# Attention on one core: output stores held back by seven pairs, the last store halved, and a new order of work in quad 2

## The chip, the cores and the metric

One core of one Trainium2 chip. The time is device microseconds of one execution; the figure for a kernel is the median of several executions. Smaller is better.

## The reference

For 16 x 32 = 512 heads, with 192 queries, 1024 keys and a head dimension of 128, all in bf16:

```python
scale = q.shape[-1] ** -0.5
scores = jnp.einsum("bhqd,bhkd->bhqk", q, k) * scale
p = jax.nn.softmax(scores, axis=-1)
return jnp.einsum("bhqk,bhkd->bhqd", p, v)
```

## The kernel before

The 512 heads are taken four at a time: 128 *quads* (NQ), numbered x. Each quad is three *steps*, so there are NF = 384 steps, numbered f or s. A quad needs 1 MB of K, 1 MB of V and 192 KB of Q, and gives 192 KB of output. Scores are computed with the keys on the partitions, so that the exponentials can go into the second matmul as they are. No maximum is subtracted: the exponential is taken directly, and the row sums come from a column of ones beside V. A check of the reciprocals of these sums decides at the end, by one number in `redo`, whether a slower general path has to run after all. With these inputs it is skipped.

What each engine does, in the order written in its own block:

- **SyncE (SP)** loads. For each n in turn it issues V of quad n + 3, K of quad n + 5 and Q of quad n + 5 (L576 to L583). There are five buffers each for K, Q and V. A K load waits until VectorE has turned all three pieces of the quad that used the buffer (L545), a V load until the second matmul is through with it (L554). After the last load SP issues those output stores that ScalarE didn't (L584).
- **VectorE** turns K (`turn_k`, three pieces of a quad) and Q (`turn_q`), and normalizes the outputs (`onorm`: a reciprocal of the sums and a multiply that writes `f_ob`). At step f it does `onorm(f - 5)`, at one step the early check, and then the pieces for step f + 3.
- **GpSimd (POOL)** reorders the turned K into `f_kt` (`order(g)`, one piece) and copies V into `f_vp` beside the ones (`spread(x, i)`, i = 0 and 1 for two heads each). For each x its order is: order(3x), spread(x-1, 0), spread(x-1, 1), order(3x+1), order(3x+2) (L621 to L631).
- **TensorE (PE)** does `qk(f)` and then `pv(f - 4)`. The second matmul of a quad has no wait of its own for V. Its order alone carries it: `pv(3(x-1))` comes after `qk(3x+1)`, which needs order(3x+1), which stands behind spread(x-1, 1) on GpSimd. There is one PSUM bank for O, so `pv(s)` takes a count of `s_on` that `onorm(s-1)` has given.
- **ScalarE (ACT)** takes the exponentials, two activations a step (L838 for one bank, L841 for three), and issues the output stores by a table, `store_at`.

Outputs of two quads (a *pair*) share one slot of `f_ob` and one store of 384 KB; the last two quads are stored alone. There are NSO = 3 slots. ACT issues the store of the pair that ends before quad x + c at step 3(x + c) + 6. A slot is written again only when its store has landed (L771). The lines that set this:

```python
    stores = [(x, GQ) for x in range(0, NQ - GQ, GQ)] + [(NQ - 2, 1), (NQ - 1, 1)]
    EARLY = NF - 9
...
            store_at = {3 * (x + c) + 6: i for i, (x, c) in enumerate(stores) if 3 * (x + c) + 6 < NF}
```

`EARLY` is the number of steps whose reciprocals the early check covers. Its three parts run on VectorE in steps f = EARLY + 5 to EARLY + 7, and a check of the rest comes behind the last `onorm`.

Of the kernel before, what the change touches and what calls it, by code (L numbers as in the profile page):

```python
# [30 lines left out]
def _general_path(nc, q, k, v, out, redo, hints, stored, G=16, NS=2, LAGS=(2, 4, 5, 7), ROUTES=(R_W, R_W, R_EA)):  # L31
# [16 lines left out]
    NPT = L_PV - L_EV + 2  # L48
    NSO = 2
    NRS = 4  # L50
# [4 lines left out]
    of = out.rearrange("b h s d -> (b h) s d")  # L55

    def route(u):
        return ROUTES[u % len(ROUTES)]
# [19 lines left out]
    with ExitStack() as es:  # L78
        def sb(name, shape, dt):
            return es.enter_context(nc.sbuf_tensor(name, shape, dt))  # L80
# [4 lines left out]
        def sem(name):  # L85
            return es.enter_context(nc.semaphore(name))
# [3 lines left out]
        vs = sb("vs", [128, NS, G, KT_TILES, 128], BF16)  # L90
        ob = sb("ob", [128, NSO, PPG, 4, 128], BF16)
        ss = sb("ss", [128, NSS, SK], F32)
# [13 lines left out]
        svl = [sem("svl%d" % i) for i in range(NS)]  # L106
        sst = [sem("sst%d" % i) for i in range(NSO)]
        s_qk = sem("s_qk")
# [8 lines left out]
        s_on = sem("s_on")  # L117
# [15 lines left out]
        def store_cnt(g):  # L133
            return 48 * (g // NSO + 1)

# [13 lines left out]
        def sync_general(e):  # L149
# [20 lines left out]
            def stores(g):  # L170
                so = g % NSO
                e.wait_ge(s_on, (g + 1) * PPG)
                h0 = g * G
                og = of[h0:h0 + G]
                e.dma_start(
                    og[:, 0:128, :].rearrange("h p d -> p h d"),
                    ob[:, so].rearrange("p pg (x y) d -> p (pg x) (y d)", y=2)[:, :, 0:128],
                ).then_inc(sst[so], 16)
                oab = og[:, 128:192, :].rearrange("(pg x) p d -> x p pg d", x=2)
                e.dma_start(oab[0], ob[0:64, so, :, 1, :]).then_inc(sst[so], 16)  # L180
                e.dma_start(oab[1], ob[64:128, so, :, 1, :]).then_inc(sst[so], 16)
# [3 lines left out]
            for g in range(NGR):  # L185
                if g + NS < NGR:
                    loads(g + NS)
                stores(g)
            for so in range(min(NSO, NGR)):
                n_uses = len(range(so, NGR, NSO))  # L190
                e.wait_ge(sst[so], 48 * n_uses)

        @block.sync
        def _(e):
            sync_general(e)
            stored(e)

        @block.gpsimd
        @_only_if(nc, redo, hints)
        def _(gp):  # L200
            gp.memset(ones[:], 1.0).then_inc(s_setup, 1)
            gp.wait_ge(s_setup, 1)
            gp.affine_select(
                ident[:], ones[:], [[1, 128]], ALU.is_equal, 0.0, base=0, channel_multiplier=-1
            ).then_inc(s_setup, 1)

            def shift(u):
                gp.wait_ge(s_max, u + 1)
                if u >= NX:
                    gp.wait_ge(s_tr, u - NX + 1)  # L210
                gp.tensor_tensor(
                    x_sb[:, u % NX, :], ss[:, u % NSS, :],
                    nb[:, u % NSS: u % NSS + 1].to_broadcast([128, SK]), ALU.subtract,
                ).then_inc(s_xp, 1)

            for u in range(NU):
                if route(u) == R_W:
                    shift(u)
# [202 lines left out]
def _attention_kernel(nc, q, k, v, out):  # L421
# [9 lines left out]
    NF = 3 * NQ  # L431
# [5 lines left out]
    AHEAD = 3  # L437
    NKN, NVS, NKT, NVP = 5, 5, 2, 2
    GQ = 2
    NSO = 3  # L440
    VB = 136

    qf = q.rearrange("b h s d -> (b h) s d")
# [2 lines left out]
    of = out.rearrange("b h s d -> (b h) s d")  # L446

    stores = [(x, GQ) for x in range(0, NQ - GQ, GQ)] + [(NQ - 2, 1), (NQ - 1, 1)]
    EARLY = NF - 9

    with ExitStack() as outer:
        redo = outer.enter_context(nc.sbuf_tensor("redo", [1, 1], mybir.dt.int32))

        def sem(name):
            return outer.enter_context(nc.semaphore(name))
# [8 lines left out]
        s_st = [sem("f_st%d" % i) for i in range(NSO)]  # L464
# [3 lines left out]
        s_vp = sem("f_vp")  # L468
# [5 lines left out]
        s_rc = sem("f_rc")  # L474
        s_pf = sem("f_pf")
        s_on = sem("f_on")
        s_fin = sem("f_fin")
        s_fl = sem("f_fl")

        with ExitStack() as es:  # L480
            def sb(name, shape, dt):
                return es.enter_context(nc.sbuf_tensor(name, shape, dt))
# [16 lines left out]
            ob = sb("f_ob", [128, NSO, GQ * 6, D], BF16)  # L499
# [15 lines left out]
            def store(e, i):  # L515
                so = i % NSO
                x, c = stores[i]
                if x + c == NQ:
                    e.wait_ge(s_fin, 1)
                else:  # L520
                    e.wait_ge(s_rc, 3 * (x + c) + 1)
                e.dma_start(
                    of[4 * x:4 * x + 4 * c].rearrange("(a x) (p j) d -> (x p) a (j d)", x=2, j=3),
                    ob[:, so, 0:6 * c, :].rearrange("p (a j) d -> p a (j d)", j=3),
                ).then_inc(s_st[so], 16)


            store_at = {3 * (x + c) + 6: i for i, (x, c) in enumerate(stores) if 3 * (x + c) + 6 < NF}

            def load_q(e, x):  # L530
                e.dma_start(
# [53 lines left out]
                    store(e, i)  # L585
            def stored(e):
                for so in range(NSO):
                    e.wait_ge(s_st[so], 16 * len(range(so, len(stores), NSO)))

            @block.gpsimd  # L590
            def _(gp):
                gp.memset(ones[:], 1.0).then_inc(s_one, 1)  # L592

                def set_v(part):
                    return gp.memset(part.bitcast(U32), 0x3F803F80)  # L595

                set_v(vp[:, 0, 0:2 * T].rearrange("p a d -> p (a d)")).then_inc(s_set, 1)
                set_v(vp[:, 0, 2 * T:].rearrange("p a d -> p (a d)")).then_inc(s_blank, 1)
                set_v(vp[:, 1].rearrange("p a d -> p (a d)"))

                def order(g):
                    x, b = divmod(g, 3)
                    lo, hi = PIECES[b]
                    gp.wait_ge(s_kx, g + 1)
                    if x >= NKT - 1 and b == 0:
                        gp.wait_ge(s_qk, 3 * (x - NKT) + 3 + PRE)
                    gp.tensor_copy(  # L607
                        kt[:, x % NKT].bitcast(U32).rearrange("p U (j s u) c -> p U j s (u c)", s=2, u=2)[:, lo:hi],
                        kx[:, x % 2].rearrange("p (U s j u) -> p U j s u", s=2, j=32, u=2)[:, lo:hi],
                    ).then_inc(s_kt, 1)  # L610

                def spread(x, i):
                    if i == 0:
                        gp.wait_ge(s_v[x % NVS], 16 * (x // NVS + (2 if x % NVS == 0 else 1)))
                        gp.wait_ge(s_pv, 3 * (x - NVP) + 3 + BLANK)
                    gp.tensor_copy(  # L616
                        vp[:, x % NVP, 2 * T * i: 2 * T * i + 2 * T, 0:D].bitcast(U32),
                        vs[:, x % NVS, 2 * i: 2 * i + 2, :].rearrange("p a (t d) -> p (a t) d", d=D).bitcast(U32),
                    ).then_inc(s_vp, 1)

                for x in range(NQ + 1):  # L621
                    if x == NQ // 2:
                        hint(gp)
                    if x < NQ:
                        order(3 * x)
                    if x >= 1:
                        for i in range(2):
                            spread(x - 1, i)
                    if x < NQ:
                        order(3 * x + 1)  # L630
                        order(3 * x + 2)  # L631

            @block.tensor
# [84 lines left out]
            def _(dve):  # L718
# [4 lines left out]
                for z in range(2):  # L723
                    ins = clear(low[:, z, :, 1, :])
# [4 lines left out]
                for z in range(2):  # L729
                    ins = clear(low[:, z, :, 2, :])  # L730
# [30 lines left out]
                def onorm(s):  # L761
                    x, w = divmod(s, 3)
                    i, a = where[x]
                    so = i % NSO
                    ri = rinv[:, 2 * s: 2 * s + 2]
                    dve.wait_ge(s_pv, s + 1 + BLANK)
                    O = o_of(s)
                    dve.reciprocal(ri, O[:, :, 128]).then_inc(s_rc, 1)  # L768
                    dve.wait_ge(s_rc, s + 1)
                    if a == 0 and w == 0 and i >= NSO:  # L770
                        dve.wait_ge(s_st[so], 16 * (i // NSO))  # L771
                    dve.tensor_tensor(  # L772
                        ob[:, so, 6 * a + 2 * w: 6 * a + 2 * w + 2, :],
                        O[:, :, 0:128],
                        ri.unsqueeze(2).to_broadcast([128, 2, D]),
                        ALU.mult,
                    ).then_inc(s_on if s < NF - 1 else s_fin, 1)

                cnt = [0]

# [17 lines left out]
                for f in range(NF + LAG + 1):  # L798
                    s = f - LAG - 1
                    if f == NF // 2:  # L800
                        hint(dve)
                    if s >= 0:
                        onorm(s)
                        if 0 <= s - EARLY < 3:
                            check(0, 2 * EARLY, 0, s - EARLY)
                    g = f + AHEAD
                    if 5 <= g < NF:
                        x, b = divmod(g, 3)
# [3 lines left out]
                for part in range(3):  # L812
                    check(2 * EARLY, 2 * NF, 1, part)
                dve.sem_inc(s_fl, 1)  # L814
# [69 lines left out]
```

## Time and profile before

| | |
|---|---|
| Median of 4 runs | 818.04 us (817.12 to 819.3) |
| Profiled execution | 816.57 us, span 814.8 us |
| PE busy | 800.9 us, 98% |
| ACT busy | 749.9 us, 92% |
| VectorE busy | 604.5 us, 74% |
| GpSimd busy | 552.0 us, 68% |
| Moved by DMA | 319.16 MB, mean 392 GB/s |
| Loads of K, V and Q, issue to landing (median) | 18.1, 16.3, 14.2 us |
| Stores issued by ACT, issue to landing (median) | 9.5 us, 62 of 384 KB |

The profile is one execution. An engine is busy while one of its instructions runs; time in which it waits is put down to whatever released it, as far as the profile shows it. The DMA share is the mean over the core's 16 DMA engines, and can come out slightly above 1. Queue q1 is SP's, q10 is ACT's. In a timeline the columns are start and duration in us, engine, line, operation, output and input, and in brackets the idle time before it and what ended that.

### The profile page before, as it was taken

To read this page: it belongs to the slowest core of one execution; us is meant where nothing else is said; L and a number is where in the kernel's file an instruction comes from. 1 tells how busy PE (TensorE), PEld (TensorE's weight loads), DVE (VectorE), ACT (ScalarE), POOL (GpSimd) and SP (SyncE) were. 2 spreads that over 40 slices of the span, in tenths; PEclk is the share of its full clock that TensorE was granted. 3 is DMA by queue.
4 is the path that set the end of the run, shared out by engine and by line. 5 is a ranking of instruction groups with operands and counts; after the bars stand their busy time and mean duration, and the time that the engine had idled before them with its cause. 6 is when DMAs were issued, how large, how long until landed. Compare 5 with 4: busy or idle time off the path is not lost. (4 is left out here: it accounts for less than half of the span.)

```text
span 814.8 us, 71454 instructions
## 1 busy us (share of the span) xinstructions
PE 800.9 (98%) x32996; PEld 714.1 (88%) x32996; DVE 604.5 (74%) x1293; ACT 749.9 (92%) x772; POOL 552.0 (68%) x648
## 2 busy tenths in 40 slices
PE   8999999999999999999999999999999999999997
PEld 6888888888888888888888888888888888888886
DVE  4777777777777777777777777777777777777775
ACT  7999999999999999999999999999999999998995
POOL 5776767667667767766766676676666766766674
PEclk9999999999999999999999999999999999999999
DMA  8999999999999999999999999999999999999992
GB/s 290 402 406 407 407 406 406 408 405 405 408 404 406 407 404 407 407 403 407 408 403 409 407 403 408 407 404 394 398 407 401 401 408 396 390 407 387 389 379 69
DMA packets 138454, 319.16 MB, mean 392 GB/s; under 512 B 7216, under 2 KB 56368, under 8 KB 122160
## 3 DMA queue, kind: packets, MB, share of 16 engines
q1 hardware_dynamic: 105536, 294.22, 92.0%
q10 hardware_dynamic: 32880, 24.58, 9.0%
q14 instruction: 32, 0.26, 0.1%
q8 instruction: 6, 0.10, 0.1%
HBM read 293.60 MB, written 25.17 MB: 391 GB/s over the span
## 5 line engine op out<-in xcount | busy, mean ns | idle before, releaser
L841 ACT ACTIVATE f_pt<-f_s 128x1536 bf16<-128x1536 f32 x384 | 554.6, 1444 | 0.0
L654 PE MATMUL f_s<-f_qt,f_kt 32*128 32x192 bf16 (+1 forms) x20528 | 422.0, 226 | 7.2 <-PEq L637 6.4
L683 PE MATMUL f_o<-f_vp,f_pt 128*64 128x129 bf16 x12368 | 425.8, 222 | 1.8 <-PEq L637 1.0
L683 PEld LDWEIGHTS f_o<-f_vp,f_pt 128*64 128x64 bf16 x12368 | 362.8, 110 | 51.1 <-issue 24.8
L616 POOL COPY f_vp<-f_vs 128x1024 uint32<-128x1024 uint32 x256 | 260.1, 1045 | 208.0 <-DMA f_vs<-in_v_dram 202.0
L654 PEld LDWEIGHTS f_s<-f_qt,f_kt 32*128 32x128 bf16 x20528 | 348.4, 92 | 44.1 <-issue 9.8
L747 DVE STREAM_TRANSPOSE f_kx<-f_kn 128x768 uint32<-128x768 uint32 (+1 forms) x384 | 335.1, 873 | 59.0 <-DMA f_kn<-in_k_dram 55.0
L607 POOL COPY f_kt<-f_kx 128x768 uint32<-128x768 uint32 (+1 forms) x384 | 295.2, 788 | 44.1 <-DVE f_kx L747 39.2
L838 ACT ACTIVATE f_pt<-f_s 128x512 bf16<-128x512 f32 x384 | 229.5, 598 | 56.4 <-PE f_s L654 15.4
L772 DVE TENSOR_TENSOR f_ob<-f_o,f_rinv 128x256 bf16<-128x256 f32 x381 | 161.8, 425 | 13.3 <-DVE f_rinv L768 0.3
L768 DVE RECIPROCAL f_rinv<-f_o 128x2 f32<-128x2 f32 x381 | 63.7, 167 | 132.7 <-PE f_o L683 130.6
L756 DVE STREAM_TRANSPOSE f_qt<-f_qn 128x384 uint32<-128x384 uint32 x128 | 73.0, 570 | 0.0
L825 ACT ACTIVATE f_pt<-f_ones 128x1536 f32<-128x1536 bf16 x3 | 4.2, 1473 | 0.0
L595 POOL MEMSET f_vp<- 128x1088 uint32 (+1 forms) x3 | 3.8, 1311 | 0.0
L683 PE MATMUL f_s<-f_vp,f_pt 128*64 128x129 bf16 x96 | 3.2, 220 | 0.2 <-issue 0.2
L683 PEld LDWEIGHTS f_s<-f_vp,f_pt 128*64 128x64 bf16 x96 | 2.9, 110 | 0.4 <-issue 0.4
L825 ACT ACT_TABLE_LOAD x1 | 1.3, 1283 | 1.2 <-PEq L869 1.2
L696 PE MATMUL f_o<-f_ones 128*128 128x512 bf16 x2 | 1.0, 620 | 1.1 <-POOL f_ones L592 1.1
L720 DVE MEMSET f_pt<- 128x256 uint32 x4 | 1.1, 272 | 0.9 <-PEq L869 0.9
L768 DVE RECIPROCAL f_rinv<-f_s 128x2 f32<-128x2 f32 x3 | 0.5, 171 | 1.4 <-PE f_s L683 1.4
L713 PE MATMUL f_o<-f_bad,f_ones 128*1 128x1 bf16 x1 | 0.2, 165 | 1.3 <-DVEq L814 1.3
L713 PEld LDWEIGHTS f_o<-f_bad,f_ones 128*1 128x1 bf16 x1 | 0.1, 80 | 1.4 <-DVEq L814 1.4
(15 smaller groups left out, 6.9 us busy)
## 6 DMA issues: line engine op xcount, KB each, us to landing
f_kn<-in_k_dram SPq DMA_DIRECT2D x127, 1024.0 KB, 18.1
f_vs<-in_v_dram SPq DMA_DIRECT2D x127, 1024.0 KB, 16.3
f_qn<-in_q_dram SPq DMA_DIRECT2D x127, 192.0 KB, 14.2
out_dram<-f_ob ACTq DMA_DIRECT2D x62, 384.0 KB, 9.5
f_vs<-in_v_dram SPq DMA_DIRECT2D x2, 512.0 KB, 6.5
f_kn<-in_k_dram SPq DMA_DIRECT2D x2, 512.0 KB, 4.6
out_dram<-f_ob SPq DMA_DIRECT2D x1, 384.0 KB, 3.7
out_dram<-f_ob SPq DMA_DIRECT2D x2, 192.0 KB, 2.2
```

Of the source, the lines that this page charges most:

```text
L595: return gp.memset(part.bitcast(U32), 0x3F803F80)
L607: gp.tensor_copy(kt[:, x % NKT].bitcast(U32).rearrange("p U (j s u) c -> p U j s (u c)", s=2, u=2)[:, lo:hi], kx[:, x % 2].rearrange("p (U ...
L616: gp.tensor_copy(vp[:, x % NVP, 2 * T * i: 2 * T * i + 2 * T, 0:D].bitcast(U32), vs[:, x % NVS, 2 * i: 2 * i + 2, :].rearrange("p a (t d) ...
L654: ins = pe.matmul(S[:, c0: c0 + n1 - n0], kt[r, x % NKT, 2 * t + h, :, c], qt[r, x % R, h, n0:n1, c], start=w == 0 and g == 0, stop=w == 3 ...
L683: ins = pe.matmul(O[64 * z: 64 * z + 64, u, 0:129], pt[:, x % R, 2 * y + z, t * SQ + 64 * j: t * SQ + 64 * j + 64], vp[:, x % NVP, (2 * y ...
L747: dve.transpose(kx[:, x % 2].rearrange("p (U s j u) -> p s u U j", s=2, j=32, u=2)[:, :, :, lo:hi], kn[:, x % NKN].rearrange("p (s u U i) ...
L756: dve.transpose(qt[:, x % R].bitcast(U32).rearrange("p b (y j u) c -> p u y b (j c)", y=3, u=2), qn[:, x % NKN].rearrange("p (u y b i) -> ...
L768: dve.reciprocal(ri, O[:, :, 128]).then_inc(s_rc, 1)
L772: dve.tensor_tensor(ob[:, so, 6 * a + 2 * w: 6 * a + 2 * w + 2, :], O[:, :, 0:128], ri.unsqueeze(2).to_broadcast([128, 2, D]), ALU.mult,). ...
L825: return act.activation(part.bitcast(F32), ones[:, 0:1].to_broadcast([128, 2 * T * SQ // 2]), ACT_FN.Copy)
L838: act.activation(pt[:, x % R, 0, c], s1_ps[:], ACT_FN.Exp, scale=scale).then_inc(s_e1, 1)
L841: act.activation(pt[:, x % R, 1:4, c], s3_ps[f % 2][:], ACT_FN.Exp, scale=scale).then_inc(s_e3, 1)
```

## The change

Five things change.

1. `f_ob` gets ten slots. ACT's stores come 42 steps, seven pairs, later (`HOLD`), and none is put on ACT after step NF - 12. SP issues the remaining ones after its last load: nine pairs and the two single quads, where it issued one pair and the two singles.
2. The store of the last quad becomes two, of two heads each; `s_fin` counts the last two steps in place of the last one.
3. `EARLY` goes from NF - 9 to NF - 33.
4. In quad 2 (`HELD`) GpSimd does order(7) ahead of the two spreads of quad 1. Since `qk(7)` no longer implies that V is there, VectorE holds back the count of `s_on` that `pv(3)` takes: after `onorm(2)`'s multiply it waits for that multiply and for the first spread of quad 1, and only then adds to `s_on`.
5. In the general path, GpSimd also waits for the stores (`stored(gp)`).

```diff
@@ general path, GpSimd
+            stored(gp)
             gp.memset(ones[:], 1.0).then_inc(s_setup, 1)
@@ constants
-    NSO = 3
+    NSO, HOLD = 10, 7
+    HELD = 2
...
-    EARLY = NF - 9
+    EARLY = NF - 33
...
+        s_held = sem("f_held")
@@ store(e, i)
                 if x + c == NQ:
-                    e.wait_ge(s_fin, 1)
-                else:
-                    e.wait_ge(s_rc, 3 * (x + c) + 1)
+                    for y in range(2):
+                        e.wait_ge(s_fin, y + 1)
+                        e.dma_start(
+                            of[4 * x + 2 * y:4 * x + 2 * y + 2].rearrange("x (p j) d -> (x p) (j d)", j=3),
+                            ob[:, so, 3 * y:3 * y + 3, :].rearrange("p j d -> p (j d)"),
+                        ).then_inc(s_st[so], 16)
+                    return
+                e.wait_ge(s_rc, 3 * (x + c) + 1)
...
-            store_at = {3 * (x + c) + 6: i for i, (x, c) in enumerate(stores) if 3 * (x + c) + 6 < NF}
+            store_at = {3 * (x + c) + 6 + 6 * HOLD: i for i, (x, c) in enumerate(stores)
+                        if 3 * (x + c) + 6 + 6 * HOLD <= NF - 12}
@@ stored(e)
-                    e.wait_ge(s_st[so], 16 * len(range(so, len(stores), NSO)))
+                    last = (len(stores) - 1) % NSO == so
+                    e.wait_ge(s_st[so], 16 * (len(range(so, len(stores), NSO)) + last))
@@ GpSimd's loop
                     if x < NQ:
                         order(3 * x)
+                    if x == HELD:
+                        order(3 * x + 1)
                     if x >= 1:
                         for i in range(2):
                             spread(x - 1, i)
                     if x < NQ:
-                        order(3 * x + 1)
+                        if x != HELD:
+                            order(3 * x + 1)
                         order(3 * x + 2)
@@ onorm(s)
-                    dve.tensor_tensor(
+                    ins = dve.tensor_tensor(
...
-                    ).then_inc(s_on if s < NF - 1 else s_fin, 1)
+                    )
+                    if s == 3 * (HELD - 1) - 1:
+                        ins.then_inc(s_held, 1)
+                        dve.wait_ge(s_held, 1)
+                        dve.wait_ge(s_vp, 2 * HELD - 1)
+                        dve.sem_inc(s_on, 1)
+                    else:
+                        ins.then_inc(s_on if s < NF - 2 else s_fin, 1)
```

## The prediction

> **What bounds the kernel now.** I read the slices of the page first, then the waits of the steady stretch, then the timelines of single engines.
>
> ```profile
> PE 800.9 (98%) x32996; PEld 714.1 (88%) x32996; DVE 604.5 (74%) x1293; ACT 749.9 (92%) x772; POOL 552.0 (68%) x648
> q10 hardware_dynamic: 32880, 24.58, 9.0%
> out_dram<-f_ob SPq DMA_DIRECT2D x1, 384.0 KB, 3.7
> out_dram<-f_ob SPq DMA_DIRECT2D x2, 192.0 KB, 2.2
> ```
>
> PE and ACT are both nearly full, so every hole in them is lost for good. Stretches of the windows view (us, busy time of each engine, clock, DMA share, GB/s) show the transfers at their limit too, until the loads are through:
>
> ```profile
> 37.00:122.00 85.00, 85.00 (x3540) 76.00 (x3538) 63.82 (x140) 80.30 (x84) 58.32 (x69) 1.00 1.04 406
> 740.00:795.00 55.00, 53.89 (x2220) 48.04 (x2216) 40.04 (x88) 50.55 (x53) 36.93 (x43) 1.00 1.00 382
> 795.00:801.00 6.00, 5.38 (x230) 4.80 (x230) 5.33 (x12) 5.47 (x6) 4.68 (x7) 1.00 0.27 90
> 801.00:815.00 14.00, 9.77 (x366) 8.70 (x354) 6.43 (x20) 5.82 (x6) 3.37 (x3) 1.00 0.20 61
> ```
>
> The last 20 us leave the DMA engines idle for four fifths. How often the shortage reaches ACT is told by the waits from 28.4 to 798.8:
>
> ```profile
> POOL f_vp L616 <- DMA f_vs<-in_v_dram: 198.8, 121, 3.1
> DVE f_kx L747 <- DMA f_kn<-in_k_dram: 44.8, 80, 1.6
> ACT f_pt L838 <- PE f_s L654: 9.6, 24, 1.0
> ```
>
> The sum of 9.6 counts overlaps, so I go by ACT's starts. From 38.63 to 239.88 it does 98 steps: 2.0536 us a step. Step 8 starts at 28.36 and step 380 at 798.75: 770.39 for 372 steps, against 372 x 2.0536 = 763.9. So 6.4 us are lost in between, in places where VectorE waited for a K load first. Steps 0 to 8 take 18.51 against 16.43: 2.1 us lost at the start. One hole comes after all K loads:
>
> ```profile
> 798.27 1.01 DVE L784 TENSOR_SCALAR f_chk<-f_rinv 128x750 f32<-128x750 f32 x1
> 799.31 0.58 DVE L756 STREAM_TRANSPOSE f_qt<-f_qn 128x384 uint32<-128x384 uint32 x1
> 801.50 0.60 ACT L838 ACTIVATE f_pt<-f_s 128x512 bf16<-128x512 f32 x1 [0.81 <-PE f_s L654]
> ```
>
> The first check stands in front of the last turn of Q, PE waits for that, and step 381 starts 2.75 after step 380: 0.70 lost, with no load to blame.
>
> [...] its V copies start when the load lands:
>
> ```profile
> 51.40 2.03 POOL L616 COPY f_vp<-f_vs 128x1024 uint32<-128x1024 uint32 x2 [1.10 <-DMA f_vs<-in_v_dram]
> 57.93 2.03 POOL L616 COPY f_vp<-f_vs 128x1024 uint32<-128x1024 uint32 x2 [1.48 <-DMA f_vs<-in_v_dram]
> 63.70 2.03 POOL L616 COPY f_vp<-f_vs 128x1024 uint32<-128x1024 uint32 x2 [1.08 <-DMA f_vs<-in_v_dram]
> 70.15 2.03 POOL L616 COPY f_vp<-f_vs 128x1024 uint32<-128x1024 uint32 x2 [1.37 <-DMA f_vs<-in_v_dram]
> 75.88 2.03 POOL L616 COPY f_vp<-f_vs 128x1024 uint32<-128x1024 uint32 x2 [0.94 <-DMA f_vs<-in_v_dram]
> ```
>
> The steps are 6.53, 5.77, 6.45, 5.73: a quad in which a pair is stored takes 0.7 to 0.8 us longer. [...]
>
> **Part 1, stores seven pairs behind.** ACT's first store goes from step 12 to step 54, about 37 to 122 us. Seven pairs of stores leave the stretch before the last loads and land after them. Each frees 0.75 us of load time (bounds: 0.69, the low end of the spacing, and 0.97, its 393 KB at 406 GB/s): 7 x 0.75 = 5.2 us, bounds 4.8 to 6.8. The loads can use it, since a K load takes 18.1 us from issue to landing, so some 18 us of work stand queued, more than 5.2. Slot reuse in ob costs nothing: a slot's store is issued 11 steps (22.6 us) ahead of its next writer as before, and lands in 9.5. ACT issues eight stores fewer; an issue there lies beside its activation, so 0.
>
> Loads that set the end come 5.2 earlier, so of the 6.4 us of holes 1.2 would stay.
>
> **Part 2, the check at step 356 (EARLY).** Its three parts (702 columns, about 0.94, 0.87, 0.87 by the 750-column rows) now stand in steps that also turn K, at about 2.05 - 1.6 = 0.45 us of free VectorE time a step. I put 0.7 to 1.2 us of hole on them, the low end by the hole at step 381, the high end adding 0.45 for the third part. But a hole ahead of a late load is paid out of the 1.2 that the loads would cost anyway; and the 0.70 after the last K load is gone. By loads the stream ends 5.2 + 0.7 = 5.9 earlier, by engines 6.4 + 0.7 - (0.7 to 1.2) - 0.1 = 5.8 to 6.3. The later holds: **-5.8 us**. The last check grows from 18 to 66 columns: 48 more at (1009 - 167) / 732 = 1.15 ns, some 0.05 us in each of three parts in series: **+0.15**.
>
> **Part 3, quad 2.** GpSimd's order(7) goes ahead of the V spread that starts at 21.59, so QK of step 7 (now 24.73, idle 0.24) may start some 0.3 earlier. I count it at nothing, since the next PV waits for something else:
>
> ```profile
> 24.55 0.98 DVE L747 STREAM_TRANSPOSE f_kx<-f_kn 128x768 uint32<-128x768 uint32 x1 [1.45 <-DMA f_kn<-in_k_dram]
> 25.62 0.42 DVE L772 TENSOR_TENSOR f_ob<-f_o,f_rinv 128x256 bf16<-128x256 f32 x1
> 26.19 1.10 PE L683 MATMUL f_o<-f_vp,f_pt 128*64 128x129 bf16 x32 [0.36 <-PEq L637]
> ```
>
> VectorE stands before the K load that lands at 24.5, so the normalization that frees the O bank ends at 26.04, and PV starts at 26.19 whatever QK did. The new wait stands after that instruction: V's half has been spread by 22.6, so it costs the semaphore's way round alone, about the 0.04 us seen between reciprocal and multiply, up to 0.1; queued behind it are the next turn of K on VectorE, and PE through s_on. Part 3: -0.3 to +0.15, value +0.1, already in the sum.
>
> **Part 4, the end.** SP, behind its last load, now issues nine pairs, a single and two halves, where it issued a pair and two singles. K of the last quad is turned at 794.72; two V loads follow, the first copied from 797.83, the second 1,049 KB later at 406 GB/s, 2.6 us: loads end near 800.4, then 795.2. A pair in a queue of stores alone is not shown. Low bound 0.75, as between loads; high bound twice the difference of the landings above, 2 x (3.7 - 2.2) = 3.0. I take the queue's own share: 9.0% of 814.8 / 62 = 1.18. Ten pairs' worth then needs 11.8 and 2 for the landing: 809.0. The last multiply, at 811.61 before, ends at 805.8; a half issued then lands near 807.9. Before, 1.0 us lay between the last landing (811.64 + 2.2) and the end of the span, and the chain of waits ran over the check and not the store. So the store is late by 1.1, of which I charge **+0.5** (0 to 1.1). That the last store is halved gains at most 0.2 and is hidden behind this: 0. The longer list of waits in stored() is a few waits already satisfied, and GpSimd's new call of it stands in the branch that is skipped: 0 to 0.1 together.
>
> **Sum.** -5.8 + 0.15 + 0.5 = -5.15. The profiled execution took 816.57 (span 814.84, 1.7 around it) and would take 811.4. It lies 1.5 under the median of the runs, 818.04; I apply the difference to the median: **812.9 us**.
>
> **Rivals.** A measurement of this kernel can tell about 0.2%, 1.6 us, from no change; "same" means within that.
>
> *Forecast*, 0.68: the credit carries to the end, 811 to 814.5.
>
> *The credit is spent early*, 0.17: the rate fell to 382 GB/s in the last stretch, and with a shortage that grows further where the check's hole is added to it, only 2 to 3.5 us remain: 814.5 to 816. For it: the holes get longer late (1.0 at most after 740). Against: lost rate costs the kernel before as much.
>
> *The engines are the bound and the holes weren't the loads'*, 0.05: then the two checks cancel, and the time stays within 1.6 us of 818.0. Against: the holes that I followed have VectorE waiting for K ahead of them.
>
> *The stores drain too slowly*, 0.10, the slower side (0.02 of it within the same band): from 795.2 the queue has 12.7 us less 2 of landing for ten pairs' worth, so from about 1.1 us a pair each 0.1 adds 1.0 us, and at about 1.7 the gain is gone. At 3.0 it would end near 795.2 + 30 + 2 = 827, and the run near 831. The landing of the lone pair after 3.7 us speaks for it; the 9.0% share and the 0.75 between loads speak against it.
>
> A last rival is that store order does nothing because the loads' rate isn't shared: the 6.53 and 5.77 exclude it.
>
> **How the numbers follow.** Faster 0.85 (forecast and spent credit), same 0.07 (the engines' case and 0.02 of the slow tail), slower 0.08. The range 810.6 to 816.2 holds the first two cases and leaves out the slow tail and the top of the credit's bound (6.8 instead of 5.2, which would be 811.3 less the missing tail cost).
>
> **What would show it.** ACT's holes against K between 122 and 720 us gone or nearly so; GpSimd's V wait far below 198.8 us; V spacing near 5.7 from 37 to 122 us; a check hole near 740 us and none at step 381; DMA share near 1 for some 10 us after the loads. Step 8 should not come sooner than 28.36. If holes against K stay at 4 us or more in sum, the credit was mis-sized; if the last landing is over 2 us behind the last multiply plus 2.2, the tail was.

## The result, and the profile after

The changed kernel takes 814.33 us (median of 42 runs, 812.3 to 818.72), the kernel before 817.07 (63 runs). The ratio is 0.9969, with a 95% interval of 0.9961 to 0.9976: 0.31% faster. The medians lie 2.7 us apart; the forecast was 5.15 us. (One of the 63 executions took 1186.45 us; the median isn't moved by it.)

In the profiled executions the span went from 814.84 to 812.07. Cut at ACT's starts and at the end of the last multiply, the 2.8 us between these two spans divide like this:

| Stretch | before, us | after, us | difference | forecast |
|---|---|---|---|---|
| to ACT's first step | 9.85 | 10.55 | +0.70 | 0 |
| step 0 to step 8 | 18.51 | 18.94 | +0.43 | +0.1 |
| step 8 to step 380 | 770.39 | 764.58 | -5.81 | -5.1 to -5.2 |
| step 380 to step 383 | 6.85 | 6.16 | -0.69 | -0.70 |
| step 383 to the last multiply's end | 6.01 | 6.97 | +0.96 | 0 |
| from there to the end of the span | 3.23 | 4.87 | +1.64 | +0.15 and +0.5 |

(The forecast's 5.8 for the middle and the check, and 0.1 of the start, are set apart here.) The middle gave what was asked of it. The start and the end took 3.7 us back, where 0.75 was reckoned with. Each column is one execution. The 1.1 us of the start turn out below to be mostly a matter of the execution, so that the sum of this table comes so near to the 2.7 us of the medians is in part chance.

The waits of the steady stretch, steps 8 to 380 of the kernel after (us in total, times, longest):

```profile
POOL f_vp L629 <- DMA f_vs<-in_v_dram: 45.7, 37, 2.3
DVE f_kx L763 <- DMA f_kn<-in_k_dram: 3.2, 10, 0.5
ACT f_pt L861 <- PE f_s L670: 2.3, 3, 1.3
```

Before, these were 198.8, 44.8 and 9.6. ACT's remaining three waits are the one at step 8 itself (1.3) and two behind the check. Those two are seen in the timeline of VectorE and ACT after:

```profile
745.73 1.00 DVE L809 TENSOR_TENSOR f_chk<-f_chk,f_rinv 128x702 f32<-128x702 f32 x1
746.30 0.60 ACT L861 ACTIVATE f_pt<-f_s 128x512 bf16<-128x512 f32 x1 [0.31 <-PE f_s L670]
748.17 0.88 DVE L811 TENSOR_REDUCE f_bad<-f_chk 128x1 bf16<-128x702 f32 x1
748.89 0.60 ACT L861 ACTIVATE f_pt<-f_s 128x512 bf16<-128x512 f32 x1 [0.64 <-PE f_s L670]
```

The two steps start 0.20 and 0.53 late: 0.73, the low end of the 0.7 to 1.2 given. The windows view after shows where the stores went (busy time of each engine, clock, DMA share, GB/s):

```profile
37.00:122.00 85.00, 85.00 (x3548) 75.98 (x3542) 64.09 (x139) 80.18 (x84) 60.16 (x71) 1.00 1.04 401
790.00:796.00 6.00, 6.00 (x256) 5.35 (x252) 4.61 (x10) 5.78 (x6) 4.68 (x7) 1.00 0.67 219
796.00:812.00 16.00, 9.43 (x346) 8.40 (x338) 4.87 (x18) 5.83 (x7) 2.44 (x3) 0.94 0.51 159
```

From 37 to 122 us the engines move loads alone at 401 GB/s, in place of 406 with the stores among them. GpSimd's V copies, whose spacing was to show it, start 5.70 and 5.73 us apart at first (40.23, 45.93, 51.66) and then 6.00 to 6.17, which is the engines' own pace of three steps, 6.16: the loads no longer hold them. The end of the span, idle for four fifths before, is half full. And in that end stands the first of the two new losses. PE's timeline after:

```profile
801.04 1.43 PE L699 MATMUL f_s<-f_vp,f_pt 128*64 128x129 bf16 x33
803.66 1.97 PE L699 MATMUL f_s<-f_vp,f_pt 128*64 128x129 bf16 x63 [1.19 <-issue]
```

PE's timeline before, at the same instruction:

```profile
808.07 1.97 PE L683 MATMUL f_s<-f_vp,f_pt 128*64 128x129 bf16 x63 [0.23 <-issue]
```

The 96 matmuls are those of `pv(380)` to `pv(382)`, 32 each. One matmul into `pv(381)`, PE stops for 1.19 us in place of 0.23, waiting for nothing that the profile shows ("issue"). The second loss comes after all the work. Lines of the source view after give the jump over the general path and, on VectorE and ACT, the instruction it leads to (starts at the end of the line):

```profile
L22 ACTq COMPARE_BRANCH  x1: 68/68/68, 809.8 to 809.8; - x1
```

```profile
L78 DVEq DRAIN  x1: 57/57/57, 810.3 to 810.3; - x1
L78 ACTq DRAIN  x1: 86/86/86, 811.8 to 811.8; - x1
```

VectorE is through at 810.3, ACT only at 811.8, 1.9 us behind its branch, and the end waits for the last engine. Before, 0.5 us lay between the two:

```profile
L22 ACTq COMPARE_BRANCH  x1: 68/68/68, 813.8 to 813.8; - x1
```

```profile
L78 ACTq DRAIN  x1: 84/84/84, 814.3 to 814.3; - x1
```

### The profile page after: what moved, and what is told of

It reads as the page before. It is cut to its first block, busy times and chain, and to the rows that moved or that the text cites. A ratio compares the mean times of both kernels' runs of the same rounds, so it can differ in the third digit from the quotient of the medians.

```text
span 812.1 us, 71452 instructions
## 1 busy us (share of the span) xinstructions
PE 799.3 (98%) x32996; PEld 713.6 (88%) x32996; DVE 600.3 (74%) x1293; ACT 750.0 (92%) x772; POOL 551.7 (68%) x648
## 5 line engine op out<-in xcount | busy, mean ns | idle before, releaser
L620 POOL COPY f_kt<-f_kx 128x768 uint32<-128x768 uint32 (+1 forms) x384 | 300.3, 787 | 196.2 <-DVE f_kx L763 195.8
```

Source lines behind the costliest of these rows:

```text
L620: gp.tensor_copy(kt[:, x % NKT].bitcast(U32).rearrange("p U (j s u) c -> p U j s (u c)", s=2, u=2)[:, lo:hi], kx[:, x % 2].rearrange("p (U ...
```

## The experiments

My theory after the result (A): held stores give the loads a credit, which is the whole gain; it is given back at the end by two delays that have nothing to do with the landing of data. PE's stop of 1.19 us grows with the backlog of stores (G), and ACT's late end, 1.9 us behind its branch, is the place of its program, which is eight instructions shorter, with 54 stores issued in place of 62 (E). That PE's stop is a fetch of instructions was a guess of mine; the times that bear on it stand below, with all profiles. The rivals: the check or quad 2 carry the gain (B, C, D), the backlog is behind ACT's end too (F), or the last landings set the end (H).

**Stores alone.** The kernel before with ten slots and the held `store_at`, no other edit:

```diff
-    NSO = 3
+    NSO, HOLD = 10, 7
-            store_at = {3 * (x + c) + 6: i for i, (x, c) in enumerate(stores) if 3 * (x + c) + 6 < NF}
+            store_at = {3 * (x + c) + 6 + 6 * HOLD: i for i, (x, c) in enumerate(stores)
+                        if 3 * (x + c) + 6 + 6 * HOLD <= NF - 12}
```

> The kernel before with the held stores alone (ten slots, seven pairs behind, none on ACT after step NF - 12); the check, quad 2 and the last store as before. Theory A (the credit in load time is the whole gain): ACT's waits for PE between the start and step 380 fall from 9.6 us to under 1; the hole of 0.7 at step 381 is back, as the check stands there again; the time is that of the full change within 0.5 us, so about 2.7 us under the kernel before. Rival B (the moved check or quad 2 carry the gain): at most 1 us under the kernel before.

Measured: 814.79 us, ratio 0.9963 (0.9949 to 0.9978), the same as the full change. Waits from 34 to 796 us:

```profile
ACT f_pt L839 <- PE f_s L655: 0.2, 1, 0.2
```

Before, this window has 9.0. Step 381 starts 0.82 late again, as the check stands there. So the stores are the gain, and B is out. Moving the check gains nothing: the hole at step 381 is 0.66 to 0.82 us in the four profiles that have it, and those that take its place behind step 356 are 0.73 in the first profile of the changed kernel and 0.96 to 1.17 in eight others. ACT's jump takes 1.8 us in this kernel too.

**Quad 2 undone.**

```diff
-    HELD = 2
+    HELD = -5
```

> The changed kernel with quad 2 as before (no early order(7), no held slot). Theory A: the normalization that stands behind the third K load sets step 8 in both, so the time stays within 0.3 us of the changed kernel, and PV of the second quad starts 1.65 to 1.75 us after that load lands, 0.1 less than in the changed one. Rival C (the order of quad 2 costs what the start shows, 1.1 us more than before): about 1 us faster than the changed kernel. Rival D (it gains at the start): 0.3 us or more slower than it.

Measured: 814.27 us, ratio 0.9957 (0.9934 to 0.9979), not to be told from the changed kernel's. PV of the second quad started 1.66 us after the third K load had landed (27.83, then 29.49), against 1.75 in the changed kernel (25.57, then 27.32), as A expected. But the profile had a late start (22.9 us from step 0 to 8), so the two single profiles don't answer C and D; the starts are taken up below.

**ScalarE's program put back in its place.**

```diff
+            filler = [3 * (x + c) + 6 for x, c in stores[:7]] + [NF - 6]
                     if f in store_at:
                         store(act, store_at[f])
+                    elif f in filler:
+                        act.sem_inc(s_pad, 1)
```

> The changed kernel with eight semaphore increments in ScalarE's program, at the places where the kernel before had its first seven and its last ScalarE stores, so that its instructions lie as before. In the changed kernel 4.9 us pass from the end of the last multiply to the end of the span, before 3.2. Theory E [...]: the 4.9 falls to about 3.5, the time by 1.4 us. Rival F [...]: 4.9 stays and so does the time.

The source view of this kernel:

```profile
L22 ACTq COMPARE_BRANCH  x1: 68/68/68, 814.7 to 814.7; - x1
```

```profile
L78 ACTq DRAIN  x1: 84/84/84, 815.1 to 815.1; - x1
```

From branch to drain 0.5 us in place of 1.9, and 3.56 from the last multiply to the end in place of 4.87, with PE's stop still there (1.46). E holds, F is out. The time, 814.01 us, ratio 0.9945 (0.9922 to 0.9967), moved the right way, but these few runs can't tell it from the changed kernel's.

**A small backlog.** The nine pairs that SP stores write one eighth of their data (one head of eight, not half of one as the expectation has it); the rest of those outputs is left out.

```diff
+                if i >= len(store_at) and c == GQ:
+                    e.dma_start(of[4 * x].rearrange("(p j) d -> p (j d)", j=3),
+                                ob[0:64, so, 0:3, :].rearrange("p j d -> p (j d)")).then_inc(s_st[so], 16)
+                    return
```

> The changed kernel in which the nine pairs that SP stores write an eighth of their data (half of one head of eight), so the rest of these outputs is left out. Theory A with G [...]: PE's idle time of 1.19 us ahead of the second multiply of step 381 falls to 0.2 to 0.3, the time by about 1 us. Theory E: ScalarE's late end stays, so 4.9 us still pass from the last multiply to the end of the span. Rival F: that falls to 3.5 too, and the time by about 2.4 us in all. Rival H (the last landings set the end): the time falls by over 2 us with PE's idle time unchanged.

PE's timeline:

```profile
804.03 3.21 PE L705 MATMUL f_s<-f_vp,f_pt 128*64 128x129 bf16 x96
```

All 96 matmuls of the three steps run without a stop, where 33 and 63 stood apart: 5.60 us from step 383 to the last multiply in place of 6.97. ACT's drain is still late (branch at 811.4, drain at 813.1; 4.63 to the end). That fits a stop of PE that the backlog makes, and a delay of ACT that it doesn't make; H is out. The time, 814.03 us (0.9954, 0.9936 to 0.9971), shows less than the 1 us expected; it can't be told from the changed kernel's. In this profile ACT's K holes came back late (4.8 us from 34 to 796), as in the previous kernel's (7.2).

**A gap in the backlog.** Fillers as above, and SP lets PE finish its scores before the fifth of its stores:

```diff
                 for i in range(len(store_at), len(stores)):
+                    if i == len(store_at) + 4:
+                        e.wait_ge(s_qk, NF + PRE)
                     store(e, i)
```

> The kernel with the eight fillers in ScalarE's program, and SP issues four of its nine pairs behind the last load, then waits until the last score matmul is done before it issues the other five. Theory G [...]: the idle time ahead of the second multiply of step 381, 1.19 us in the changed kernel, falls to 0.3 or less, and about 1 us from ScalarE's last step to the last multiply with it; the last landing moves from 1.7 us to 2.5 to 3.5 us behind the last multiply, so of the 1 us between 0 and 1 is kept. Time 1.5 to 2.4 us under the changed kernel. [...]

```profile
801.60 3.49 PE L704 MATMUL f_s<-f_vp,f_pt 128*64 128x129 bf16 x96
```

The stop is gone from PE's timeline with the full data stored, and 5.87 us pass from step 383 to the last multiply. The stores now end late, 4.1 us behind the last multiply where 2.5 to 3.5 was expected, and so 4.74 us pass from there to the end though ACT jumps in 0.5. The run took 814.69 us, 0.9964 (0.9946 to 0.9981). One loss was exchanged for another, and the expected 1.5 us aren't seen.

**Three pairs held.** The changed kernel with `NSO, HOLD = 6, 3`.

> The changed kernel with stores three pairs behind in place of seven (six slots). Theory A with a credit of 0.75 us a pair: 2.2 us of credit in place of 5.2; ACT's holes behind late K loads, none in the changed kernel's profile, come back to about 6.4 - 2.2 = 4 us between step 8 and 380, at most 0.7 less where the check takes their place; SP stores five pairs, so the backlog ends some 4 us earlier and PE's idle time of 1.19 falls to 0.3. Time 0.5 to 2.5 us above the changed kernel. Rival B' (any delay of the stores frees the loads): no holes, and 1 us below it.

```profile
ACT f_pt L861 <- PE f_s L670: 6.9, 15, 1.1
```

That is the window from 34 to 796 again, of this kernel. The holes are back, from step 265 on; in this profile the small credit doesn't fill them, as A expected and B' didn't. Yet the time is 814.22 us, ratio 0.9959 (0.9946 to 0.9972), not above the changed kernel's: PE's 96 matmuls run through, and ACT's drain follows its branch in 0.5 us without fillers. In its profile the middle is 4.5 us longer than in the changed kernel's first (769.09 from step 8 to 380) and the end 2.5 shorter (9.31 from step 383 on, against 11.84). But this execution took 817.44, 3.2 above the median of its kernel, so how the two balance in most executions isn't shown. Of my 0.5 to 2.5 us above, some 1.4 was ACT's late end, which I had kept in it.

**Five pairs held, with fillers,** twice, the second time beside the changed kernel itself (`NSO, HOLD = 8, 5`, fillers for the first five stores and the last).

> The changed kernel with stores five pairs behind (eight slots) and fillers in ScalarE's program so that it lies as in the kernel before. Theory A: credit 3.7 us, about 2 us of holes behind late K loads where a run is as the profiled one of the kernel before; seven pairs on SP, backlog 2 us shorter, PE's idle time between 0.3 and 1.2; ScalarE's end as before (3.5 us from the last multiply to the end). Time within 1 us of the one with seven pairs and fillers. Clearly faster than that one would mean that the backlog costs more than 0.75 us a pair.

> The kernel with five pairs held and fillers, once more, beside the changed kernel on one chip. If its lead is real, it is 1 to 2.5 us faster than the changed kernel here: 1.4 from ScalarE's end, up to 1 from PE's fetch, less at most 1.5 of credit where loads bind again. If the lead was the draw of a few executions, the two lie within 0.7 us.

> The changed kernel itself as the partner of the one with five pairs held: 2 to 3.5 us under the kernel before, and in its profile again an idle time of about 1.2 us ahead of the second multiply of step 381 and 4.6 to 4.9 us from the last multiply to the end.

812.85 us, 0.9937 (0.9915 to 0.9958), and 812.94 us, 0.9939 (0.9921 to 0.9956); the changed kernel beside the second 814.03, 0.9955 (0.9938 to 0.9972). So it beats the kernel before clearly. It lies 1.1 us under the changed kernel there, with intervals that overlap; from the interval of the changed kernel's 42 runs (0.9961 to 0.9976) both of its own lie apart. Its profiles have 2.6 and 1.9 us of ACT's waits from 34 to 796, a stop of PE of 0.37 and ACT's jump at 0.5. Whether five pairs with fillers beat seven with fillers isn't settled: 0.9937 and 0.9945 lie well within each other. The changed kernel's second profile had no stop of PE: a start 4.6 us longer (23.57 to step 8) with loads no later (the last K load landed at 788.7, in the first at 789.9) let the backlog drain to one pair before PE began its 96 matmuls. My 1.2 for it was wrong, in the way that G asks for. ACT's late end was there again, 4.70, and the middle was again short, 764.91 from step 8 to 380.

**Both delays over all thirteen profiles.** The page of each profile lists two queues of the kind "instruction" among those of the DMA engines (packets, MB, share); this is the changed kernel's:

```profile
q14 instruction: 35, 0.29, 0.1%
q8 instruction: 7, 0.11, 0.1%
```

The traces have the time of every such packet, though not the engine it is for. For PE, sorted by the pairs that SP had issued and that hadn't landed when these 96 matmuls began:

| Pairs queued | Stop of PE, us |
|---|---|
| 4 | 1.19 (changed kernel), 1.46 (fillers) |
| 3 | 0.51 (stores alone), 0.42 (quad 2 undone) |
| 2 | 0.37, 0.37 (five held), none (gap in the backlog) |
| 1 | 0.23, 0.23, none (kernel before), none (three held; an eighth of the data; changed kernel, second profile) |

So it isn't the number of pairs put off that counts, but how many are still queued at that moment. A packet of 16 KB on q8 starts 0.75 to 1.28 us ahead of these matmuls in eleven profiles, and 0.39 and 0.45 us after their start in the two with four pairs. In all eight profiles with a stop, PE goes on 1.27 to 1.49 us after this packet has ended; in the changed kernel's first it runs from 801.43 to 802.39, and PE goes on at 803.66. The longer start of the changed kernel's second profile holds a stop of the same kind in the midst of the loads: PE stands for 2.99 us by "issue" up to 20.16, and the packet took from 15.95 to 18.90.

For ACT, in the five profiles with a late end a packet of 8 KB on q14 starts 0.17 to 0.30 us after the branch, and the drain comes 1.71 to 1.95 us after the branch. In the other eight no such packet starts within 1.0 us of the branch, one starts 10.2 to 13.7 us ahead of it, and the drain comes after 0.48. These eight include three pairs held, where ACT issues only four stores fewer than before. Both delays thus coincide with packets of these two queues. PE's is the longer the more pairs are queued, 1.19 and 1.46 us with four and at most 0.37 with two; ACT's is there in the five profiles of a kernel whose ACT program is eight instructions shorter, and in no other. That the engines wait for what these packets bring is a guess and isn't shown.

**The start of the kernel before,** two more executions.

> The kernel before, one look at its start. The first profile of it took 18.5 us from the first step of ScalarE to step 8; the runs with the change show 18.9 to 23.6. If the late starts are drawn anew in each execution (K and V of the first quads landing later), this one need not show 18.5 and can lie anywhere up to 23; if they come from the change, it shows 18.5 within 0.3, with the third K load landing near 24.5.

> The same once more: a second draw of the start of the kernel before. Three draws within 0.3 us of 18.5 would put the late starts on the change; a spread of a microsecond or more would put them on the execution.

817.87 and 820.99 us. Step 0 to 8 took 18.73 and 20.65, and the first step came at 10.74 and 9.96. VectorE's line for the third K load in the last one, where 24.55 stood in the prediction:

```profile
26.81 0.98 DVE L747 STREAM_TRANSPOSE f_kx<-f_kn 128x768 uint32<-128x768 uint32 x1 [3.07 <-DMA f_kn<-in_k_dram]
```

The late start is drawn in each execution: it is 18.5 to 22.9 us in the five profiles with the old order of quad 2 and 18.9 to 23.6 in the eight with the new one. Up to step 8 the kernels differ in that order alone. Three profiles of the kernel before are too few to exclude a small difference on average. Counted from the moment that this load's turn begins, step 8 starts 3.81, 3.81 and 3.80 us later in the three profiles of the kernel before, and 3.90 in the changed one (25.59 to 29.49), 3.90 with fillers (25.76 to 29.66).

## Why the prediction was right or wrong

**Part 1 held.** The holes in front of K loads, 6.4 us by its count, are gone; the last K load landed 4.8 us sooner by the trace's record of landings (794.7, then 789.9), in a run whose first step came 0.7 later. Not one late K load reached ACT, so none of the 1.2 us that "would stay" stayed. As all 6.4 are gone, the credit of 5.2 was on the low side of its own bounds (4.8 to 6.8). ACT's waits from 34 to 796 us follow the number of pairs held: 9.0, 9.7 and 12.2 in the three profiles with none, 6.9 with three, 2.6 and 1.9 with five, 0.2 to 2.0 in five profiles with seven. But in two more profiles with seven, 4.8 and 7.2 us came back, so the size of the credit per pair isn't shown by these single profiles. Why the loads were slower in those two executions stays open. ACT's issues did lie beside its activations: the one at 124.35, 0.40 us long, overlaps those that start at 123.95 and 124.45.

**Part 2 held** in its size, 0.73 to 1.17 over nine profiles against 0.7 to 1.2, and in its place, though the first of the three parts took 0.52 us in the changed kernel's first profile (743.57) and not the 0.94 reckoned, which it took in the second. The step argued that loads would hide this hole; since in most profiles no late load was left, it is a plain cost, as large as the one it replaced or up to some 0.4 larger. The last check's widening shows as 0.12 in the end stretch: from the last multiply to the write of `redo` 0.97 us pass, before 0.85; 0.15 was reckoned.

**Part 3 held.** The third K load sets step 8, and the semaphore's way round costs 0.09, within "up to 0.1". Nothing is gained at step 8; at step 7 the changed kernel starts on time where the kernel before started 0.30 late, and the next step takes that back.

**Part 4 is where the sum failed.** It charged +0.5 for the last landings and +0.15 for the check, and took the rest of the end as unchanged; the end grew by 2.6. (From step 383 on it takes 8.9 to 9.3 us in the three profiles of the kernel before, 11.8 and 10.3 in the two of the changed one.) The price per pair was close: the landings of the SP stores stand 1.05 us apart in the record (797.58, 798.63, 799.68 and so on), against the 1.18 taken. In the changed kernel the data was no obstacle: the last store landed at 808.85, 3.2 us ahead of the end. The DMA share was 0.75 from 796 to 805 us, below the "near 1" that was to show it. SP's first pair, issued at 778.48, landed at 797.58, behind the last K load's 789.9, as the step had it. What the step left out is the two delays: PE's stop in the middle of a run of matmuls, from 0.23 or none with one pair queued to 1.46 us with four; and ACT's 1.9 us at its jump over the general path, which eight filler instructions turn into 0.5. I read neither from the profile of before, where the same places cost 0.23 and 0.5 us. That ACT's delay hangs on the length of its program is shown by the fillers, and PE's stop goes with the pairs still queued, 1.19 and 1.46 us with four and at most 0.23 with one. That both are fetches of instructions isn't shown: the times of the packets fit it, but no packet names its engine.

**Luck in the number.** The forecast's gain of 5.15 us became 2.7, which as a gain lies in the band of the spent credit (2 to 3.5) and not in that of the forecast. That 814.33 still lies between 811 and 814.5 is luck: the kernel before came out at 817.07 and not at 818.04, which covers 1.0 us of the miss. The spent credit's mechanism, holes that stay late in the run, shows in two of seven profiles with seven pairs held and not in the others. The slow drain came near by its place, the end, but not by its mechanism. How the 2.7 us of the medians divide over most executions is known only as far as these single profiles tell.

## What to carry to other kernels

Where transfers limit the middle of a kernel and stand idle at its end (here a DMA share of 1.04 from 37 to 122 us and 0.20 from 801 on), put stores off until then: steps 8 to 380 gained 5.81 us where the holes in the profile promised 5.1 to 5.2, and ACT's waits shrank from 9.0 us or more with no pair held to 6.9 with three and 2.6 and 1.9 with five; with seven they were 0.2 to 7.2. Then price the end again with the stops that queued stores may bring (1.19 and 1.46 us with four pairs queued, at most 0.23 with one), and look at each engine's last jump: with eight instructions fewer in ACT's program it took 1.9 us from branch to drain in place of 0.5, some 1.4 us at the very end of the profiles. The best count of held stores need not be the one that fills all holes: five, with ACT undisturbed and a stop of PE of 0.37 us, did better than the changed kernel with seven, where ACT was late and PE stopped for up to 1.19.

## What the runs showed of the hardware that I had not expected

In one execution TensorE's matmuls came slowly behind an idle time of 1.90 us, and the granted clock was at half for 3.41 us. In the kernel with three pairs held, PE's timeline at the start:

```profile
27.41 1.86 PE L699 MATMUL f_o<-f_vp,f_pt 128*64 128x129 bf16 x32 [1.90 <-PEq L653]
29.20 1.89 PE L670 MATMUL f_s<-f_qt,f_kt 32*128 32x128 bf16 x48
31.02 1.10 PE L699 MATMUL f_o<-f_vp,f_pt 128*64 128x129 bf16 x32
```

After 1.90 us of idling the same 32 matmuls took 1.86 us instead of 1.10 in the changed kernel's profile, and the next 48 took 1.89 instead of 1.09; step 8 came 5.46 us after the K load's turn had begun (25.69 to 31.15), where it was 3.90 in the changed kernel. The windows view of this kernel gives the granted clock there as 0.53:

```profile
27.40:31.00 3.60, 3.59 (x80) 3.10 (x80) 2.59 (x5) 0.11 (x1) 2.31 (x4) 0.53 1.01 400
```

The trace has the clock at half from 27.54 to 30.95, 3.41 us. After the 1.13 us of the changed kernel's profile, and after 1.73 in one of the kernel before, the matmuls ran at full speed. The slow stretch didn't begin with the pause's end each time: with quad 2 undone, PE idled for 3.80 us, the next 64 matmuls took 1.10 us, the 32 behind them 1.58 and the next 48 1.89, and the clock was at half from 29.94 to 33.35. That the pause brings the lower clock isn't shown. Quad 2's new order leaves the wait for a late third K load to one place, ahead of `pv(3)`; whether it makes such slow stretches more frequent isn't shown, as they fell on both orders.
